# A linear-attention block: z computed inside the G stage, one memset on another engine, and one weight load in two parts

## The chip, the cores and the metric

The kernel runs on one core of one Trainium2 chip. The metric is the time of one execution on the device, in microseconds (us); less is better. A kernel counts as faster or slower only from 2% on (about 4.2 us here).

The engines are named as in the profile: PE is TensorE (PEld its weight loads), DVE is VectorE, ACT is ScalarE, POOL is GpSimd, and SP is SyncE, which here only issues DMA transfers. ACT issues a few DMA transfers too; its queue appears in the profile as q10, that of SP as q1.

## The reference

For x of 2048 x 640 in bf16 the result is the sum of three terms: x, a linear attention over the layer norm of x, and a two-layer GELU network over the same layer norm.

```python
def attention(x, wqkv, wo):           # H = 32 heads of Dh = 20
    q, k, v = ...                     # x @ wqkv, split by head
    phi = lambda t: jnp.where(t > 0, t + 1, jnp.exp(t)) + 1e-6
    pq, pk = phi(q), phi(k)
    kv  = jnp.einsum("bhsd,bhse->bhde", pk, v)
    z   = jnp.einsum("bhsd->bhd", pk)              # sum of phi(k) over the tokens
    num = jnp.einsum("bhqd,bhde->bhqe", pq, kv)
    den = jnp.einsum("bhqd,bhd->bhq", pq, z)[..., None] + 1e-6
    return (num / den).transpose(...).reshape(B, S, D) @ wo

def network(x, w1, b1, w2, b2):       # F = 1536
    return gelu(x @ w1 + b1) @ w2 + b2

xn = layernorm(x)
out = x + attention(xn, wqkv, wo) + network(xn, w1, b1, w2, b2)
```

## The kernel before

The kernel writes its instructions down through a small planner: `Pl.ins(engine, function, reads, writes)`. From the reads and writes the planner works out which semaphores each instruction waits for. Each engine runs its instructions in the order in which they were written down. `take(n)` hands out PSUM banks in a ring of eight; whoever takes a bank waits until its last reader is done.

The order of the stages on PE is: filler matmuls on zeros while the first loads arrive; W1 products with GELU (layer 1 of the network); K (with phi on ACT and DVE); G, the product of xn and phi(K), in five blocks f; Q chunk 0; z; KVT; Q chunks 1 and 2; M = KVT x Wo; Q chunk 3; then the output stage.

The loads at the start. W1 comes in four quarters of 480 KB; the first is issued on ACT's queue, the others on SP's, between the tiles of x:

```python
        dma_x(0, 1)                                                   # SP
        dma_w("scalar", b1tmp[:], B_b1.rearrange("(a p) -> a p", p=P), r_b1tmp)
        dma_w1(0, "scalar")                                           # first W1 quarter, ACT queue
        dma_x(1, 1)
        dma_w1(1)                                                     # second W1 quarter, SP queue
        dma_x(2, 1)
        dma_w1(2)
        # ... (cut)
```

The first products of layer 1, for token tile 0. They come in two groups: k = 0, 1 first, then k = 2, 3, 4. Both groups wait for the whole first quarter of W1:

```python
        def h_first(jbs):
            bs = [take(1) for _ in jbs]
            for (ks, res) in (((0, 1), r_xnTA), ((2, 3, 4), r_xnT[0])):
                for jb, b in zip(jbs, bs):
                    Pl.ins("tensor", [...matmuls for k in ks...],
                        reads=[r_W1[jb * P // FW], res], writes=[B_[b]])
            # ... (GELU, cut)
```

From the end of K to M. `KVT` and `GTb` lie in the memory of W1, so the memset and the G copies wait until layer 1 has read W1:

```python
        Pl.ins(v, lambda e: e.memset(KVT, 0.0), writes=[r_KVT] + r_W1)     # v is VectorE
        for f in range(DT):
            b = take(2)
            # ... 32 matmuls of G block f, and its copy to GTb on ScalarE (cut)

        # token sum on VectorE: zsum = PK[0] + PK[1] + ... + PK[15], fp32, then split in two bf16 parts zhl
        # ... (cut; 15 adds, a cast, a subtraction)

        q_chunk(0)
        z_step()      # 10 matmuls with N = 1; then DVE copies z and makes five ZB tiles
        kvt_step()    # 25 matmuls; then DVE masks and evicts five KVT tiles
        q_chunk(1)    # 5 units: 5 matmuls each, exp on ACT, then two DVE instructions (phi)
        q_chunk(2)
        m_step()      # 5 pairs of banks, 16 matmuls each, evicted by ACT
        q_chunk(3)
```

## Time and profile before

| What | Where it is read | Value |
|---|---|---|
| time, median of 3 runs | the runs | 210.89 us (210.71 to 210.95) |
| span of the profiled run | page | 209.0 us |
| PE busy | page | 204.9 us (98%) |
| first W1 products start | PE timeline | 6.84 us |
| first W1 quarter lands | DMA issues | 5.2 us after its issue at 1.46, so 6.7 |
| z products | chain | 0.36 us at 109.24 |
| M products, 80 matmuls | PE timeline | 121.91 to 125.67 = 3.76 us |
| token sum ends | DVE timeline | 99.92 us |

From the page of the kernel before: the busy time of each engine, and the chain of work that ended last.

```profile
PE 204.9 (98%) x1599; PEld 141.0 (67%) x1599; DVE 108.8 (52%) x227; ACT 75.1 (36%) x142; POOL 20.2 (10%) x61
...
PE 92%; DVE 6%; issue 1%; DVEq 0%
```

PE is almost always busy and makes up almost the whole chain. A change to another engine can only gain where that engine makes PE wait. The only such place inside the kernel is around M. Here is the PE timeline from the end of Q chunk 2 (columns: start, duration, engine, line, operation, tensors, shape, count, and in brackets the idle time before it and what ended it):

```profile
121.91 1.29 PE L545 MATMUL ps<-Wo,W 128*32 128x320 bf16 x32
123.38 0.75 PE L545 MATMUL ps<-Wo,W 128*32 128x320 bf16 x16 [0.18 <-DVE PQ L466]
124.38 1.29 PE L545 MATMUL ps<-Wo,W 128*32 128x320 bf16 x32 [0.24 <-DVE PQ L466]
125.60 2.57 PE L509 MATMUL ps<-xnT,Wqkv 128*128 128x512 bf16 x11
```

Eighty M matmuls (L545) come in three runs with gaps between them. The first 32 and the last 32 take 1.29 us each, that is 0.040 us for one, so 80 without a gap would take 3.22 us. They take 3.76, so about 0.54 us is lost. The releaser is the phi eviction on DVE (L466), which frees the banks. DVE is behind because z and KVT were put before its phi work. The chain in order of time (start, duration, what) shows it:

```profile
109.24 0.36 PE ps L517 x10
109.61 1.29 PE ps L529 x20
...
110.92 0.17 DVE z_sb L521
...
111.11 0.24 DVE ZB L523
...
112.42 0.22 DVE W L533
...
114.28 0.21 DVE ek L464
...
123.54 0.70 DVE PQ L466
...
124.38 1.29 PE ps L545 x32
```

After the z products (L517) and the KVT products (L529) it is DVE that goes on without a break: z copy, five ZB products, five KVT evictions (L533), ten phi pairs (L464 and L466), up to the last M matmuls.

At the start of the kernel, PE runs from the fillers (L298) over the transposes (L375, L303) into the first W1 products (L385) without a wait for a DMA:

```profile
6.34 0.45 PE L375 MATMUL ps<-ident,xn_tm 128*128 128x128 bf16 x3
6.73 0.18 PE L303 MATMUL ps<-ident,b1tmp 12*128 12x12 bf16 x1
6.84 1.22 PE L385 MATMUL ps<-xnT,W 128*128 128x128 bf16 x15
```

The quarter of W1 landed at about 6.7 us and was wanted at 6.84.

### The profile page before, as it was taken

Reading aid. Unit: us, or ns where it says so; the run is one execution under the profiler, and the core shown is the slowest. Engines: PE = TensorE matmul, PEld = TensorE weight load, DVE = VectorE, ACT = ScalarE, POOL = GpSimd, SP = SyncE. Lnnn points to the kernel's source line nnn. Section 1 sums busy time; section 2 is a strip of 40 time slices with the busy share of each in tenths; the row PEclk is TensorE's granted clock in tenths of the full one; section 3 lists DMA queues with packets and bytes.
Section 4 is the critical chain, followed back from the end, with each engine's and each line's share of the span. In section 5 each row is a group of like instructions: output and inputs, shape, how many; then the busy total and the mean of one; then the engine's idle time right before and its main releaser. Section 6 shows DMA issues by size and latency. Waiting matters only on the chain.

```text
span 209.0 us, 3950 instructions
## 1 busy us (share of the span) xinstructions
PE 204.9 (98%) x1599; PEld 141.0 (67%) x1599; DVE 108.8 (52%) x227; ACT 75.1 (36%) x142; POOL 20.2 (10%) x61
## 2 busy tenths in 40 slices
PE   7999999999999999999999999999999999999995
PEld 2799987444457777777756565577777777777775
DVE  4589970000008888999178975478633522523322
ACT  2689887666676444111253576100000000000000
POOL 3245568200000000000000000000000000000000
DMA  6999668997000000000000000591120111001001
GB/s 164 348 349 112 105 129 130 376 332 260 3 0 0 0 0 3 0 3 0 0 0 5 0 0 3 193 313 57 63 59 32 58 42 55 31 31 35 31 34 61
DMA packets 22507, 17.86 MB, mean 85 GB/s; under 512 B 9176, under 2 KB 22488, under 8 KB 22488
## 3 DMA queue, kind: packets, MB, share of 16 engines
q1 hardware_dynamic: 21808, 17.11, 29.1%
q10 hardware_dynamic: 680, 0.49, 0.9%
q8 instruction: 12, 0.20, 0.4%
q14 instruction: 7, 0.06, 0.1%
HBM read 12.62 MB, written 2.62 MB: 73 GB/s over the span
## 4 chain that ended last, share of the span: by engine, by line
PE 92%; DVE 6%; issue 1%; DVEq 0%
PE ps L617 33%; PE ps L355 25%; PE ps L487 10%; PE ps L476 10%; PE ps L509 5%; DVE PQ L466 3%; PE ps L298 2%; PE ps L653 2%; DVE ek L464 1%; DVE W L533 1%; PE ps L529 1%; PE ps L545 1%; DVE ZB L523 1%; PE ps L555 1%; PE ps L385 1%
## 5 line engine op out<-in xcount | busy, mean ns | idle before, releaser
L355 PE MATMUL ps<-xnT,W 128*128 128x128 bf16 (+2 forms) x435 | 52.0, 282 | 0.0
L617 PE MATMUL ps<-W,HG 128*128 128x320 bf16 x360 | 51.4, 299 | 0.0
L355 PEld LDWEIGHTS ps<-xnT,W 128*128 128x128 bf16 x435 | 35.6, 98 | 15.6
L617 PEld LDWEIGHTS ps<-W,HG 128*128 128x128 bf16 x360 | 35.1, 98 | 14.2 <-issue 0.4
L359 ACT ACTIVATE HG<-ps,b1c 128x128 bf16<-128x128 f32 (+2 forms) x87 | 40.1, 493 | 12.4 <-PE ps L355 10.3
L464 DVE TENSOR_SCALAR ek<-ek 128x512 bf16<-128x512 bf16 (+1 forms) x36 | 11.0, 305 | 42.7 <-ACT ek L463 41.6
L636 DVE TENSOR_TENSOR out_sb<-ps,xnT 128x640 bf16<-128x640 f32 x15 | 12.4, 825 | 36.2 <-PE ps L617 36.1
L463 ACT ACTIVATE ek<-ps 128x512 bf16<-128x512 f32 (+1 forms) x36 | 23.2, 645 | 20.4 <-PE ps L509 11.2
L617 PE MATMUL ps<-Msb,PQ 128*128 128x320 bf16 x150 | 22.5, 299 | 0.0
L509 PE MATMUL ps<-xnT,Wqkv 128*128 128x512 bf16 x100 | 22.1, 379 | 0.0
L476 PE MATMUL ps<-Wqkv,xnT 128*128 128x320 bf16 x160 | 21.9, 299 | 0.0
L487 PE MATMUL ps<-xPK,xn_tm 128*128 128x320 bf16 x160 | 21.9, 299 | 0.0
L476 PEld LDWEIGHTS ps<-Wqkv,xnT 128*128 128x128 bf16 x160 | 15.7, 98 | 6.2
L487 PEld LDWEIGHTS ps<-xPK,xn_tm 128*128 128x128 bf16 x160 | 15.7, 98 | 6.1
L617 PEld LDWEIGHTS ps<-Msb,PQ 128*128 128x128 bf16 x150 | 14.6, 98 | 5.7
L509 PEld LDWEIGHTS ps<-xnT,Wqkv 128*128 128x128 bf16 x100 | 11.6, 117 | 9.6 <-issue 0.2
L466 DVE SCALAR_TENSOR_TENSOR PQ<-ps,ek 128x512 bf16<-128x512 f32 x20 | 13.8, 692 | 2.1
L311 DVE BATCH_NORM_STATS2 stats<-xPK 128x6 f32<-128x320 bf16 x32 | 13.6, 466 | 2.3 <-DMA xPK<-in_A_x_dram 2.3
L466 DVE SCALAR_TENSOR_TENSOR xPK<-ps,ek 128x640 bf16<-128x640 f32 x16 | 13.2, 824 | 1.7
L497 DVE TENSOR_TENSOR Msb<-Msb,xPK 128x640 f32<-128x640 f32 x14 | 11.6, 825 | 0.5
L491 ACT ACTIVATE W<-ps 128x640 bf16<-128x640 f32 x5 | 3.5, 704 | 18.2 <-PE ps L487 14.6
L321 POOL TENSOR_TENSOR rstd<-aggr,mhalf 128x1 f32<-128x1 f32 x16 | 9.1, 568 | 8.9 <-DVE aggr L319 8.9
(68 smaller groups left out, 93.7 us busy)
## 6 DMA issues: line engine op xcount, KB each, us to landing
xnT<-in_A_x_dram SPq DMA_DIRECT2D x4, 640.0 KB, 6.2
Wqkv<-in_A_wqkv_dram SPq DMA_DIRECT2D x3, 800.0 KB, 6.7
out_dram<-out_sb SPq DMA_DIRECT2D x15, 160.0 KB, 1.8
W<-in_B_w_dram SPq DMA_DIRECT2D x1, 1920.0 KB, 15.3
W<-in_B_w_dram SPq DMA_DIRECT2D x3, 480.0 KB, 7.0
xPK<-in_A_x_dram SPq DMA_DIRECT2D x2, 640.0 KB, 9.5
Wo<-in_A_wo_dram SPq DMA_DIRECT2D x1, 800.0 KB, 10.5
xPK<-in_A_x_dram SPq DMA_DIRECT2D x4, 160.0 KB, 4.2
```

The lines of the kernel that those rows point to most:

```text
L311: Pl.ins(v, lambda e: e.bn_stats(stats[:, s, 6 * h:6 * h + 6], x_in[:, t, h * HW:(h + 1) * HW]), reads=[r_x[t]], writes=[r_stats[s][h]])
L355: Pl.ins("tensor", [(lambda e, k=k: e.matmul(bank(b, 0, w), W1[:, k, jb * P:(jb + 1) * P], xnT[:, k, tok], start=(k == 0), stop=(k == DT - ...
L359: Pl.ins("scalar", lambda e: e.activation(HG[:, jb, tok], bank(b, 0, w), ACT.Gelu_apprx_tanh, bias=b1c[:, jb:jb + 1]), reads=[B_[b], r_b1c ...
L463: Pl.ins("scalar", lambda e: e.activation(e2, src, ACT.Exp), reads=br, writes=[r_ek[s]])
L464: Pl.ins(v, lambda e: e.tensor_scalar(et, et, 1.0, 1e-6, ALU.min, ALU.add), reads=[r_ek[s]], writes=[r_ek[s]])
L466: Pl.ins(v, lambda e: e.scalar_tensor_tensor(out=d2, in0=src, scalar=0.0, in1=e2, op0=ALU.max, op1=ALU.add), reads=br + [r_ek[s]], writes= ...
L476: fns.append(lambda e, k=k, h=h, b=b, t=t: e.matmul(bank(b + h, 0, HW), xnT[:, k, t * P:(t + 1) * P], Wqkv[:, k, D + h * HW:D + (h + 1) * ...
L487: Pl.ins("tensor", [(lambda e, t=t, h=h, b=b, f=f: e.matmul(bank(b + h, 0, HW), xn_tm[:, t, f * P:(f + 1) * P], PK[:, t, h * HW:(h + 1) * ...
L497: Pl.ins(v, lambda e, t=t: e.tensor_tensor(out=zsum, in0=zsum, in1=PK[:, t, :], op=ALU.add), reads=[r_PK[t], r_zsum], writes=[r_zsum])
L509: Pl.ins("tensor", [(lambda e, k=k, j=j, b=b: e.matmul(bank(b), Wqkv[:, k, j:D:DT], xnT[:, k, cc], start=(k == 0), stop=(k == DT - 1))) fo ...
L617: return lambda e: e.matmul(bank(b + h, 0, HW), l, r[:, h * HW:(h + 1) * HW], start=(i == 0), stop=(i == JT + DT - 1))
L636: Pl.ins(v, lambda e: e.tensor_tensor(out=halves(out_sb[:, s, :]), in0=pair(b), in1=halves(x_res[:, t, :]), op=ALU.add), reads=B_[b:b + 2] ...
```

## The change

It wants to (1) take the z work out of DVE's way before M, by computing z inside the G stage, ahead of the last G block; (2) make the token sum end early enough for that, by zeroing KVT on GpSimd instead of VectorE; (3) start the first W1 products earlier, by loading the first W1 quarter as two DMA transfers, k = 0, 1 first.

```diff
+        r_W1a = R_("W1_0a")
...
-        dma_w1(0, "scalar")
+        dma_w("scalar", W1[:, 0:2, 0:FW], w1v[:, 0:2, 0:FW], r_W1a)
+        dma_w("scalar", W1[:, 2:DT, 0:FW], w1v[:, 2:DT, 0:FW], r_W1[0])
         dma_x(1, 1)
         dma_w1(1)
...
-                        reads=[r_W1[jb * P // FW], res], writes=[B_[b]])
+                        reads=[r_W1a if res is r_xnTA else r_W1[0], res], writes=[B_[b]])
...
-        Pl.ins(v, lambda e: e.memset(KVT, 0.0), writes=[r_KVT] + r_W1)
+        Pl.ins(g, lambda e: e.memset(KVT, 0.0), writes=[r_KVT] + r_W1)
...  (z_step and the token sum are now defined here; their instructions are unchanged)
+        token_sum()
         for f in range(DT):
             b = take(2)
+            zbank = (b + 3) % 8        # z_step uses this bank and takes none from the ring
+            if f == DT - 1:
+                z_step()
...
         q_chunk(0)
-        z_step()
         kvt_step()
```

## The prediction

> **What bounds the kernel now.** TensorE: the page gives PE 98% busy, the chain that ended last is 92% PE. DVE is on that chain only from 110.9 to 124.2 us. By stretches, PE is unbroken from 6.9 to 121.8 us; its one gap is 121.8 to 125.6 (3.38 busy of 3.80), the M products. Most of what the change touches limits nothing.
>
> **The wait at stake.** Chain: KVT products end at 110.90; then DVE without a break: z copy 0.17, five ZB products (to 112.42), five KVT evictions (to 114.28), ten phi pairs at 0.997 us to 124.24. PE supplies a phi unit every 1.08 us, so DVE starts late and has not caught up when the M products need the banks. These, 80 matmuls, last 121.91 to 125.67 = 3.76 us; the first and last 32 took 1.29 each, so without waits 80 take 3.22. Stall: about 0.54 us (the waits name 0.4, on the phi eviction).
>
> **Parts, costed.**
> 1. *z earlier.* 1.5 us of DVE work moves from 110.9 to about 100, where DVE is idle (5.67 us before 105.59). KVT evictions then start near 111 and phi near 112.8, not 114.2; phi follows PE's supply and ends near 123.4, about when the fourth M pair wants its bank. Stall left: 0 to 0.1. Gain 0.4 to 0.55 us. The ten z matmuls (0.36 us of PE) are moved, not removed. The bank ring loses one take, but pairs shift by two, so later conflicts stay.
> 2. *Is z ready?* The token sum ends at 99.92; PE reaches the fifth G block at 82.11 + 4 x 4.346 = 99.49. Without the DVE memset (1.39 us at 84.43) it ends near 98.6: no PE stall. The memset move makes this possible; alone it is worth nothing.
> 3. *GpSimd memset.* From 512 bf16 in 0.526 us and 140 in 0.215 I estimate 2.8 us for 3200, from 60.4 (last reader of W1) to 63.2; nothing needs it before 86.5. The Trainium skill ("SBUF — State Buffer", Who interferes with whom) says that a VectorE op in a 2-port mode and GpSimd block each other fully; the first such op starts at 63.16, so at most tenths, absorbed (phi takes 1.16 us of DVE per 1.36 of PE).
> 4. *W1 quarter in two.* The 480 KB on the ACT queue land 5.2 us after issue at 1.46, so about 6.7; the first products start at 6.84, held by the transposes ahead of them, not by W1: gain 0 to 0.1. The second part is needed at 7.38 and should land at 6.7 to 7.1: the skill ("DMA: Bandwidth & Descriptors", Queues, rings and completion order) says that each DMA engine takes turns between queues by packet, so splitting inside one queue should not change its share. The extra issue (0.4 us) delays ACT before its table load; ACT is next needed at 6.83. Net -0.1 to +0.2.
>
> **Sum.** 210.89 - 0.5 = 210.4 us; 8 in 10 between 209.9 and 210.8. Faster by over 2%: 0.01; within 2%: 0.98; slower by over 2%: 0.01.
>
> **What would show it.** z products between 99.4 and 100 without a PE gap; M products within 3.2 to 3.35 us; KVT evictions from about 111; a GpSimd memset of about 2.8 us near 60.4; first W1 products still at 6.8 to 6.9; output stage unchanged.
>
> **What would make it wrong.** The second W1 DMA landing after 7.4 (PE waits, +0.3 or more); the memset holding up DVE for microseconds; the token sum not ending before 99.5; an M pair still waiting.

## The result, and the profile after

Ratios below are computed as the mean time of one kernel's fast runs over the mean of the other's in the same rounds, so they are not quite the ratio of the medians quoted.

| | before | after |
|---|---|---|
| runs | 6 | 6 |
| median, us | 210.87 | 211.2 |
| lowest to highest, us | 210.71 to 211.03 | 210.3 to 215.13 |
| all runs, us | 210.95 210.89 210.71 211.03 210.85 210.75 | 213.84 215.13 210.89 210.3 211.44 210.97 |
| mean granted clock of the two runs above 213 | none | 0.992 (213.84), 0.984 (215.13) |

Fast runs against fast runs the ratio is 1.0002, with a 95% interval of 0.998 to 1.0023: the same. But the changed kernel scatters over 4.8 us, where the kernel before scatters over 0.3. The lowest run, 210.3, is the predicted time almost exactly; the others lie above it by 0.6 to 4.8 us. The prediction, 209.9 to 210.8, does not hold the median.

The profiled run was one of the long ones. In the changed kernel the M products are L553, the z products L490, the G matmuls L516, the W1 products L387 and L357, the memset L485. The part that the prediction was about went as predicted. PE around M:

```profile
125.46 3.27 PE L553 MATMUL ps<-Wo,W 128*32 128x320 bf16 x80
128.66 0.63 PE L528 MATMUL ps<-xnT,Wqkv 128*128 128x512 bf16 x2
```

All 80 M matmuls in one piece, 3.27 us. The z products (L490) run ahead of the last G block, and the chain has no gap around them (start, duration, what):

```profile
85.67 17.39 PE ps L516 x128
103.06 0.36 PE ps L490 x10
103.42 4.37 PE ps L516 x32
```

From the first K matmul to the last eviction of the chain it was 206.68 - 60.38 = 146.30 us before and is 209.74 - 63.94 = 145.80 us now: 0.50 us gained.

The start is where the time came back, and more. From the page, busy times and chain, in answer to those of before:

```profile
PE 206.0 (97%) x1599; PEld 142.4 (67%) x1599; DVE 107.9 (51%) x226; ACT 75.3 (36%) x142; POOL 22.9 (11%) x62
...
PE 91%; DVE 4%; DMA 3%; ACTq 0%; issue 0%; DVEq 0%
```

DMA has entered the chain with 3%, and DVE fell from 6 to 4%. The PE timeline at the start shows where:

```profile
6.42 0.18 PE L305 MATMUL ps<-ident,b1tmp 12*128 12x12 bf16 x1
6.56 0.49 PE L387 MATMUL ps<-xnT,W 128*128 128x128 bf16 x6
9.31 1.14 PE L387 MATMUL ps<-xnT,W 128*128 128x128 bf16 x9 [2.26 <-DMA W<-in_B_w_dram]
10.25 0.74 PE L341 MATMUL ps<-ident,xn_tm 128*128 128x128 bf16 x5
```

The second group of W1 products (L387, x9) starts at 9.31 us, after 2.26 us in which PE waited for the second part of the W1 quarter. The chain from the second group of W1 products on (L385 and L355 before, L387 and L357 after; start, duration, what), first of the kernel before, then of the changed one:

```profile
7.38 0.68 PE ps L385 x9
...
8.34 3.60 PE ps L355 x55
...
15.52 1.51 PE ps L355 x27
```

```profile
1.90 7.37 DMA W<-in_B_w_dram
...
9.31 1.14 PE ps L387 x9
...
10.99 4.50 PE ps L357 x55
...
19.07 0.95 PE ps L357 x17
```

Before, the large stretch of layer 1 (the last piece of each view; its length and count are cut off there by the end of the view's window) is reached at 15.52 us, after at 19.07: 3.55 us later. The wait explains 9.31 - 7.38 = 1.93 us of this. The other 1.62 us lie in the matmuls after the wait: nine W1 products take 1.14 us where they took 0.68, five transposes (left out above) 0.53 where they took 0.28, the 55 products after them 4.50 where they took 3.60. The table of stretches shows why (columns: stretch, then length, busy time and instruction count of each engine, then the granted clock of PE, the DMA share and GB/s):

```profile
core 0: us, PE busy (x) PEld busy (x) DVE busy (x) ACT busy (x) POOL busy (x), PEclk, DMA share, GB/s
9.30:11.00 1.70, 1.69 (x17) 1.69 (x18) 0.00 (x0) 1.01 (x3) 0.00 (x0) 0.51 1.09 347
11.00:15.50 4.50, 4.50 (x59) 4.38 (x58) 2.81 (x8) 3.34 (x10) 1.55 (x4) 0.81 1.07 360
```

For 1.7 us after the wait the mean granted clock was 0.51, in the next 4.5 us 0.81. The clock record of the trace says where it changed: it was half from 9.33 to 12.75 us, for 3.41 us, and full on either side. The same columns for these 3.41 us and the 3.41 us before them:

```profile
5.92:9.33 3.41, 1.15 (x14) 0.67 (x13) 0.82 (x3) 0.56 (x2) 0.21 (x1) 1.00 1.03 337
9.33:12.74 3.41, 3.41 (x33) 3.41 (x34) 1.61 (x5) 1.85 (x6) 0.25 (x2) 0.50 1.08 351
```

Half of 3.41 us is 1.7 us (an estimate of the loss), close to the 1.62 found above. In the kernel before the clock was 1.00 from 7.4 to 13.6 us. 3.55 us lost at the start, less 0.50 gained at M, makes 3.05, and the spans differ by 212.0 - 209.0 = 3.0 us.

So the profiled run is explained by its own trace. Two questions were open. Is the late second part the change's doing or chance? And why does it land so late, when it was issued only 0.4 us after the time at which the whole quarter used to be issued?

### The profile page after: what moved, and what is told of

The parts are those of the page before. It is cut to its first block, busy times and chain, and to the rows that moved or that the text cites. A ratio compares the mean times of both kernels' runs of the same rounds, so it can differ in the third digit from the quotient of the medians.

```text
span 212.0 us, 3973 instructions
## 1 busy us (share of the span) xinstructions
PE 206.0 (97%) x1599; PEld 142.4 (67%) x1599; DVE 107.9 (51%) x226; ACT 75.3 (36%) x142; POOL 22.9 (11%) x62
## 4 chain that ended last, share of the span: by engine, by line
PE 91%; DVE 4%; DMA 3%; ACTq 0%; issue 0%; DVEq 0%
PE ps L624 33%; PE ps L357 25%; PE ps L516 10%; PE ps L478 10%; PE ps L528 7%; DMA W<-in_B_w_dram 3%; DVE PQ L468 3%; PE ps L660 2%; DVE ek L466 1%; PE ps L537 1%; PE ps L553 1%; PE ps L563 1%; PE ps L387 1%; PE ps L341 1%; ACTq L235 0%
## 5 line engine op out<-in xcount | busy, mean ns | idle before, releaser
L357 PE MATMUL ps<-xnT,W 128*128 128x128 bf16 (+2 forms) x435 | 52.9, 286 | 0.0
L357 PEld LDWEIGHTS ps<-xnT,W 128*128 128x128 bf16 x435 | 36.6, 100 | 15.6
L516 PE MATMUL ps<-xPK,xn_tm 128*128 128x320 bf16 x160 | 22.1, 299 | 0.0
L516 PEld LDWEIGHTS ps<-xPK,xn_tm 128*128 128x128 bf16 x160 | 15.6, 98 | 6.0
```

The source lines that it names most:

```text
L357: Pl.ins("tensor", [(lambda e, k=k: e.matmul(bank(b, 0, w), W1[:, k, jb * P:(jb + 1) * P], xnT[:, k, tok], start=(k == 0), stop=(k == DT - ...
L516: Pl.ins("tensor", [(lambda e, t=t, h=h, b=b, f=f: e.matmul(bank(b + h, 0, HW), xn_tm[:, t, f * P:(f + 1) * P], PK[:, t, h * HW:(h + 1) * ...
```

## The experiments

Theory A: the second W1 transfer lands late, because it is issued after the SP queue has issued its own W1 quarter and shares the DMA engines with it; the wait that this makes eats what z gains, and where it is long PE also loses its clock. Rivals: the z move itself brings the scatter (B); two transfers cost more than one by themselves, whatever the order (A2); landing times are chance, whatever the queue (A3). In the first round A and B were set against each other, in the second the order against A2 and A3, in the third the low clock.

All outputs are right. The table gives every time measured, with how many of the runs had a mean granted clock below 0.998; the last column is from the profiled execution alone.

| kernel | runs | mean | lowest to highest | low clock | PE's wait for the first W1 quarter |
|---|---|---|---|---|---|
| after (first set) | 6 | 212.09 | 210.30 to 215.13 | 2 | 2.26 |
| after_again | 6 | 212.17 | 210.39 to 213.92 | 3 | 1.95 |
| one_dma | 6 | 210.26 | 209.99 to 210.72 | 0 | 0.95 |
| split_only | 6 | 212.26 | 210.80 to 214.14 | 2 | 0.45 |
| z_dve_memset | 6 | 211.44 | 210.58 to 213.41 | 1 | 1.46 |
| memset_only | 5 | 210.86 | 210.73 to 210.99 | 0 | below 0.2 |
| late_single | 6 | 213.32 | 211.68 to 214.70 | 4 | 1.73 |
| late_again | 6 | 213.99 | 211.83 to 215.43 | 5 | 1.60 |
| late_fill | 6 | 212.97 | 212.37 to 213.66 | 0 | 0.56, after 2.12 of filler |
| w1b_sp | 6 | 210.51 | 210.23 to 210.93 | 0 | none |
| sp_order | 5 | 210.12 | 209.89 to 210.31 | 0 | none |
| before_sp | 6 | 210.72 | 210.53 to 210.83 | 0 | none |
| sp_again | 6 | 210.14 | 209.91 to 210.58 | 0 | none |

The kernel before, run next to each of the three groups, had means of 210.86, 210.93 and 210.94 (11 runs each, lowest 210.44, highest 211.28 but for one run of 212.74 with a clock of 0.992).

A run is called slow here when it is over 1.5% above the fastest of the same kernel. With one core there is no other die to compare with, so the label says nothing of the cause, and some runs at 0.992 carry the label fast.

### one_dma: the change without the split

```diff
-        dma_w("scalar", W1[:, 0:2, 0:FW], w1v[:, 0:2, 0:FW], r_W1a)
-        dma_w("scalar", W1[:, 2:DT, 0:FW], w1v[:, 2:DT, 0:FW], r_W1[0])
+        dma_w1(0, "scalar")
-                        reads=[r_W1a if res is r_xnTA else r_W1[0], res], writes=[B_[b]])
+                        reads=[r_W1[jb * P // FW], res], writes=[B_[b]])
```

> The change with the W1 quarter loaded by one DMA again (z and memset stay). Theory A (the second W1 DMA lands late and eats the gain of z): first W1 products at 6.8 to 6.9 without a wait on W1, M products 3.2 to 3.35 us, time 210.3 to 210.45 in all runs, none slow, spread below 0.3 us; ratio to before about 0.9977. Rival B (the z move itself brings the slow runs or gains nothing): 210.9 or more, or some runs above 213.

Measured: 209.99 to 210.72, median 210.22, none at a low clock, ratio to before 0.9971 (0.9958 to 0.9984). M products 3.27 us. B falls: with z moved and the split undone, the gain is there, and in these six runs the scatter is gone. (It is not gone for good: z_dve_memset below, with the same single transfer, has one run of 213.41 at a clock of 0.992.) One part of the expectation was wrong: in the profiled run (210.72) the quarter did not land at 6.7 but 6.1 us after its issue at 1.45, and PE waited 0.95 us. Even one transfer lands late at times.

### split_only: the kernel before with the split alone

```diff
-        dma_w1(0, "scalar")
+        dma_w("scalar", W1[:, 0:2, 0:FW], w1v[:, 0:2, 0:FW], r_W1a)
+        dma_w("scalar", W1[:, 2:DT, 0:FW], w1v[:, 2:DT, 0:FW], r_W1[0])
-                        reads=[r_W1[jb * P // FW], res], writes=[B_[b]])
+                        reads=[r_W1a if res is r_xnTA else r_W1[0], res], writes=[B_[b]])
```

> The kernel before with only the W1 quarter in two DMAs. Theory A: second part lands after 7.4 us (up to about 9.3), PE waits for W1; times scatter from 210.9 to over 215, mean about 0.5 us or more above before, and M products still 3.7 us. Rival B: 210.9 in all runs, W1 not waited for.

Measured: 210.80 to 214.14, median 211.92; the ratio to before is 1.0061 (1.0019 to 1.0104), in which 213.88, labelled fast, counts although its clock was 0.992. The four runs at full clock have a mean of 211.39, 0.53 us above the 210.86 of before. In the profile the second part landed at 7.5 us and PE waited 0.45; that was the fastest of the six runs. The scatter comes with the split and without z. In the change, the loss of about 0.5 at full clock happens to be as large as the gain of about 0.5 from z: by this chance the ratio of the fast runs came out at 1.0002.

### after_again: the changed kernel a second time

No edit.

> The changed kernel once more, for a second profile and five more times. Theory A: times scatter by 1 us or more (210.3 to 215), the landing of the second W1 DMA in the profile differs from 9.27 us and the span of this profile follows it: span about 208.5 plus the wait for W1 plus the time lost at the lower clock. Rival B: same time as one_dma.

Measured: 210.39 to 213.92, three of six runs at a low clock; the three others have a mean of 210.75. In this profile the second part landed 7.6 us after its issue, PE waited 1.95 us and started the second group at 9.52. The stretch from there to the large stretch of layer 1 lasted 19.28 - 9.52 = 9.76 us, the same as 19.07 - 9.31 = 9.76 in the first profile, and 1.62 longer than before. The span was 212.2 us, and the expected sum is 208.5 + 1.95 + 1.62 = 212.1. The scatter repeats.

### z_dve_memset and memset_only: what the engine of the memset is worth

The first is one_dma with the memset back on VectorE, the second is the kernel before with the memset on GpSimd. The edit is the same line in both, in opposite directions:

```diff
-        Pl.ins(g, lambda e: e.memset(KVT, 0.0), writes=[r_KVT] + r_W1)
+        Pl.ins(v, lambda e: e.memset(KVT, 0.0), writes=[r_KVT] + r_W1)
```

> As one_dma, but the KVT memset back on DVE (token sum starts 1.3 us later). The token sum then ends near 99.9 us and PE, which reaches the z products at about 99.5, waits 0.4 to 0.5 us: time about 210.75, 0.4 us above one_dma. If the memset's engine does not matter: equal to one_dma within 0.1 us.

> The kernel before with the KVT memset on GpSimd and nothing else. It should gain nothing: 210.9, ratio 0.999 to 1.001, M products still about 3.7 us, token sum ending 1.3 us earlier; the memset about 2.8 us on GpSimd.

Measured: z_dve_memset has a mean of 211.04 over its five runs at full clock, against 210.26 for one_dma: 0.78 more, where 0.4 was expected. The PE timeline of z_dve_memset shows the wait; the z products are L489 and stood idle for the token sum on DVE (L505):

```profile
102.52 0.56 PE L489 MATMUL ps<-onesb,Msb 128*128 128x1 bf16 x10 [0.48 <-DVE Msb L505]
102.94 2.33 PE L515 MATMUL ps<-xPK,xn_tm 128*128 128x320 bf16 x16
```

From the first K matmul to the start of the output stage's last tile it takes 204.71 - 62.92 = 141.79 us, and in one_dma 202.03 - 60.92 = 141.11: 0.68 us. Of this, 0.42 is the time by which the sum comes too late (17.81 us after K's end, where PE arrives after 17.39), 0.05 passes until PE starts, and the z products then take 0.56 us where the chain of one_dma has 0.36. The direction is as expected, the size was taken too small. The rest of the 0.78 may be the scatter of W1, which this kernel keeps.

memset_only: 210.73 to 210.99, ratio 0.9996 (0.9984 to 1.0008). M products from 122.17 to 125.96 with both gaps, 3.79 us. The token sum ended at 98.57 instead of 99.92, and nothing waited for it. So the memset on GpSimd is worth nothing alone and 0.7 to 0.8 us under the z move: it is a condition for the gain and no gain of its own. It took 2.77 us there, on VectorE 1.39:

```profile
60.79 2.77 POOL L483 MEMSET W<- 128x3200 bf16 x1 [22.36 <-PE ps L355]
```

and in the kernel before:

```profile
84.43 1.39 DVE L483 MEMSET W<- 128x1600 uint32 x1 [0.28 <-issue]
```

The Trainium skill ("VectorE: DVE Perf Modes", Zero memsets can be issued as uint32) says that a VectorE memset takes a cycle per element, and that a zero memset of 2-byte elements can go out as half as many uint32. The trace agrees on the form: the row of VectorE has 1600 uint32 for the 3200 bf16, and the row on GpSimd, which has 3200 bf16, takes twice as long. No run here has the bf16 form on VectorE, so none shows what the uint32 form saves there.

### late_single: one transfer, issued just after SP's

The kernel before, with one more small load on ACT's queue ahead of the W1 quarter, so that the quarter is issued a little later (the cut leaves out the new tile and the b1 transpose, which waits for the extra load too):

```diff
+        dma_w("scalar", b1dup[:], B_b1.rearrange("(a p) -> a p", p=P), r_b1dup)
         dma_w1(0, "scalar")
```

> The kernel before (W1 quarter in one DMA), with a second copy of the small b1 load issued on the ACT queue ahead of it, so that the quarter is issued about 0.6 us later, after the SP queue has issued its own W1 quarter. Theory A1 (being issued behind the SP queue's W1 load is what makes it land late): lands at 8.5 to 9.5 us, PE waits 2 us or more, some runs at a clock of 0.992, mean 212 or more. Rival A2 (two DMAs cost more than one, by themselves): landing moves by the 0.6 us of issue only, 7.2 to 8.4, mean 211.0 to 211.5.

The issue moved by less than planned, from 1.46 to 1.79 us, but that was enough: SP issued its W1 quarter at 1.72. The landing moved to 8.6 us in the profile, PE waited 1.73 (2 or more was expected), and the mean was 213.32, with four of six runs at a low clock. A2, which allowed a mean of 211.0 to 211.5, falls: there is only one transfer, it was issued 0.33 us later, and the time rose by more than in the split kernels. (The landing alone would not decide: in late_again below, the same kernel, it was 8.1 us, which A2 allows.) What is left is the order: which of the two W1 transfers is issued first. One small doubt stays: the extra load of 3 KB is itself ahead of the quarter in ACT's queue, and no run had it there with the quarter still issued first. The DMA queues between 3 and 5 us (columns: queue and kind, packets, MB, share of the 16 engines' time), first of the kernel before, then of late_single:

```profile
DMA packets 629, 0.48 MB, mean 240 GB/s; under 512 B 17, under 2 KB 629, under 8 KB 629
...
q10 hardware_dynamic: 505, 0.38, 76.7%
q1 hardware_dynamic: 124, 0.10, 15.7%
```

```profile
DMA packets 569, 0.44 MB, mean 219 GB/s; under 512 B 33, under 2 KB 569, under 8 KB 569
...
q1 hardware_dynamic: 446, 0.36, 78.4%
q10 hardware_dynamic: 123, 0.08, 14.4%
```

ACT's queue (q10) moved 505 of 629 packets when its quarter was issued first, and 123 of 569 when it was issued 0.07 us after SP's. In the changed kernel, from 4 to 7 us, when the second part should have come in, ACT's queue moved 370 packets and SP's (q1) 648:

```profile
q1 hardware_dynamic: 648, 0.52, 65.7%
q10 hardware_dynamic: 370, 0.27, 28.1%
```

That is nearly the share that ACT's queue had in the kernel before in the same 3 us, 418 packets to 807. The difference is in the end of the transfer: after 7 us ACT's queue had no packet left to move in the kernel before, but 62 of its 696 in the changed kernel, and up to 9.3 us these came among 911 of SP's. It is the last tenth of the load that makes it land late.

The prediction leaned on the Trainium skill ("DMA: Bandwidth & Descriptors", Queues, rings and completion order), which says that each DMA engine takes turns between the queues packet by packet. A packet there is a group of descriptors, typically 9 to 17 and at most 64, drained from one queue before the next has its turn. The profile may count something smaller: in its trace the quarter is 640 packets of 768 bytes, 40 for each of 16 engines (an estimate), and one packet of the page could hold many of these. So uneven counts over 2 us neither confirm even turns nor speak against them, and no run shows the turns themselves.

### w1b_sp: the second part on SP's queue, ahead of SP's own quarter

```diff
         dma_w("scalar", W1[:, 0:2, 0:FW], w1v[:, 0:2, 0:FW], r_W1a)
-        dma_w("scalar", W1[:, 2:DT, 0:FW], w1v[:, 2:DT, 0:FW], r_W1[0])
         dma_x(1, 1)
+        dma_w("sync", W1[:, 2:DT, 0:FW], w1v[:, 2:DT, 0:FW], r_W1[0])
         dma_w1(1)
```

> The changed kernel with the second W1 part issued on the SP queue, ahead of that queue's own W1 quarter. A1: it lands before 7.4 us, PE hardly waits for W1, no run at a lower clock, time 209.9 to 210.3. A2: still late (8 us or more) in some runs, times scatter up to 213.

Measured: 210.23 to 210.93, mean 210.51, none at a low clock; the part landed 4.1 us after its issue, where it had taken 7.4, and all fifteen first W1 products ran without a wait, from 6.48 us on. So two transfers are not late as such: this one, ahead of SP's quarter, was under way for 3 us less. (It changed its queue too; that the order counts on one and the same queue rests on late_single.) Four of the six runs, up to 210.93 and one of them by 0.01 only, are above the expected 209.9 to 210.3. The profile shows a wait of 0.16 us for the second quarter instead; whether that is all of it, one profile cannot say.

### sp_order, before_sp and sp_again: one transfer, in order, in one queue

sp_order is one_dma with the first quarter on SP's queue, ahead of the second. before_sp is the same edit on the kernel before. sp_again is sp_order once more, on the same chip as before_sp.

```diff
-        dma_w1(0, "scalar")
         dma_x(1, 1)
+        dma_w1(0)
         dma_w1(1)
```

> As one_dma, but the whole first W1 quarter goes to the SP queue, third after two x tiles and ahead of the second W1 quarter; it is issued about 0.3 us later than in one_dma. A1 (sharing with and order against the SP queue's loads decides): it lands at 6.2 to 6.9 in spite of the later issue, against 7.5 and 8.0 in the two profiles with one DMA and memset or z changes; time 209.9 to 210.2 with a spread below 0.3 us. Rival A3 (landing is just late by chance, whatever the queue): as one_dma, 210.0 to 210.7, landing 6.7 to 8.

> The kernel before with only the issue order changed: first W1 quarter in one DMA on the SP queue, after two x tiles and ahead of the second quarter. If order and sharing decide the landing: no wait for W1, first W1 products at 6.5 to 6.9, time 210.5 to 210.7 with a spread of at most 0.3 us (before scatters over 0.8), M products still 3.7 us. The z part is absent, so about 0.5 us above sp_again. Rival: if the order is worth nothing, 210.9 as before.

> sp_order once more, beside before_sp on one chip: 209.9 to 210.3, all runs at clock 1.0, ratio to before 0.996 to 0.997, 0.4 to 0.55 us below before_sp (the z part alone).

Measured: sp_order 209.89 to 210.31, ratio 0.9961 (0.9948 to 0.9973); sp_again 209.91 to 210.58, ratio 0.9961 (0.9929 to 0.9993); before_sp 210.53 to 210.83, ratio 0.9989 (0.9961 to 1.0018). The highest run of sp_order is 0.1 above what was expected, that of sp_again 0.3, and four of the six of before_sp are up to 0.13 above. The last two ratios count the run of before at 212.74, whose clock was 0.992; without it before has a mean of 210.76, so that sp_again is 0.3% below it and before_sp level with it. The median of before_sp, 210.76, is not lower than the 210.79 of before on that chip; what it lacks is the tail of before, whose eleven runs there include 211.21 and 212.74. So the order does not make the kernel faster when all goes well; it seems to keep it from getting slower: before_sp keeps within 0.30 us, though six runs are few for something seen once in eleven. The z part alone, sp_again against before_sp, is 210.72 - 210.14 = 0.58 us; 0.4 to 0.55 was expected.

The PE timeline of sp_order at the start:

```profile
6.40 0.18 PE L304 MATMUL ps<-ident,b1tmp 12*128 12x12 bf16 x1
6.51 1.22 PE L386 MATMUL ps<-xnT,W 128*128 128x128 bf16 x15
7.57 0.44 PE L340 MATMUL ps<-ident,xn_tm 128*128 128x128 bf16 x5
```

Fifteen W1 products in one piece at 6.51 us, with no wait for W1, although the quarter was issued 0.3 us later than in one_dma. A3 falls for this load: in three profiles of three, with the quarter ahead of SP's, PE did not wait for it. What remains is that the second quarter now comes close: in sp_again PE's weight loads waited 0.3 us for it at about 8 us.

All runs together say more of the order than one kernel can. Where the quarter, or its second part, was issued behind SP's quarter (after, after_again, split_only, late_single, late_again), 16 of 30 runs had a low clock. Where it was ahead on ACT's queue (one_dma, z_dve_memset, memset_only and the 33 runs of before), it was 2 of 50, and ahead on SP's queue (w1b_sp, sp_order, before_sp, sp_again) none of 23.

sp_order is the version that beats both kernels: 0.4% below the kernel before, then 0.3 to 0.4%. It is under 2%, so it counts as the same. That it beats one_dma (ratio 0.9971, on another chip) is not shown.

### late_fill and late_again: is it the wait that lowers the clock?

late_fill is late_single with nine matmuls on zeros put where PE would wait. late_again is late_single once more, on the same chip.

```diff
         b1_step()
+        filler(9)
```

> late_single with nine extra 512-column matmuls on zeros (1.94 us of PE) put between the b1 transpose and the first W1 products, so that PE is not idle while W1 is on its way. If PE's idle time is what lowers the granted clock: clock 1.0 in all runs, time 211.3 to 212.8, about 1 us below late_again in its slow runs. Rival (the low clock comes of itself): clock 0.992 as often as in late_again, times up to 214.7.

> late_single once more, beside late_fill: mean near 213, about two in three runs at clock 0.992; runs at clock 1.0 between 211.5 and 212.5.

Measured: late_fill 212.37 to 213.66, all six at 0.999 or 1.000. late_again 211.83 to 215.43, five of six at 0.992 or below; those five have a mean of 214.42. In its profile the quarter landed as late as in the changed kernel, and PE had 0.56 us of idle time before it instead of 2.26. The PE timeline, and the stretches at the same times as those of the changed kernel above:

```profile
6.70 2.12 PE L301 MATMUL ps<-warm 128*128 128x512 bf16 x9
9.37 1.01 PE L388 MATMUL ps<-xnT,W 128*128 128x128 bf16 x15 [0.56 <-DMA W<-in_B_w_dram]
```

```profile
9.30:11.00 1.70, 1.63 (x29) 1.63 (x30) 0.30 (x1) 0.91 (x4) 0.00 (x0) 1.00 1.10 335
11.00:15.50 4.50, 4.50 (x65) 4.28 (x63) 3.42 (x11) 3.90 (x12) 1.55 (x4) 1.00 1.07 361
```

The clock stays at 1.00. So the low clock is not something that befalls the runs from outside: the idle time of PE at the start brings it. Three of the six times are above the expected range, up to 213.66. Nine fillers also hold PE back when W1 is early: the best run, 212.37, is above the 211.83 of late_again at full clock. The filler is a measuring tool here, not a remedy.

The length of the wait alone does not decide. In single profiles a wait of 1.46 us (z_dve_memset) was followed by a low clock, while waits of 1.60 and 1.73 (late_again, late_single) were not followed by any loss. The clock records in the traces say more. In the three profiles with a low clock it was half for one step of 3.41 us: from 9.33 us (after), 10.12 (after_again) and 7.86 (z_dve_memset). In the 3.41 us that ended there PE was busy for only 1.15, 1.46 and 1.57 us; z_dve_memset had another gap, of 0.62 us, in them. The records of the profiles without a loss run in the same steps (their first entry lasts 204.8 us, 60 steps). In the step that holds the wait PE was busy for 1.68 us (late_single), 1.81 (late_again), 2.12 (one_dma) and 2.37 (split_only). So in these seven profiles the three with the least PE work in one step lost half the clock in the next. Seven profiles do not place the limit, and the same wait can cost the clock or not, depending on where the steps fall.

This also fits with the few sizes in which the low clock comes. A mean of 0.992 over 212 us is a loss of 0.008 x 212 = 1.7 us, one step at half the clock, and 0.984 would be two (estimates; no profile has a clock of 0.984). The 18 low-clock runs here have 0.991, 0.992 or 0.984.

## Why the prediction was wrong, point by point

- **PE bounds the kernel, and only M has a wait inside it: right.** M products went from 3.76 to 3.27 us (predicted 3.2 to 3.35).
- **z earlier gains 0.4 to 0.55: right.** 0.50 by the traces of before and after; 0.58 by runs of sp_again against before_sp.
- **z is ready in time because the memset left VectorE: right.** The z products started at 103.06 in the profile after, which is 17.39 us after the end of K (85.67), without a gap. With the memset on VectorE PE waits and 0.7 to 0.8 us are lost.
- **The GpSimd memset takes 2.8 us and disturbs nothing: right.** 2.76 us, from 64.08 to 66.84. The skill's rule that GpSimd and a 2-port VectorE instruction block each other ("SBUF — State Buffer", Who interferes with whom) was hardly put to the test: VectorE's first instruction of that stage started at 66.71, as late after the first K matmul as before (2.77 and 2.78 us), and took 0.33 us as before. The two spans overlap by 0.13 us, and spans on POOL are rough, so no run here shows the rule or a breach of it.
- **The W1 quarter in two, "Net -0.1 to +0.2": this is the step that failed.** The prediction said that the second part "should land at 6.7 to 7.1". It landed at 9.27, 9.47 and 7.5 us in three profiles with the split. In the profiled run this term of the sum was 3.55 us, of which 1.93 was the wait and 1.62 the clock; at full clock it is about 0.5 us (split_only against before), which is the whole gain of z. Two things were missed. First, the argument was about the share of a queue, which hardly changed (36% of the packets against 34% from 4 to 7 us), while the load landed 2.6 us later; what counted was the order of issue against the other queue's W1 transfer, and the split moved 288 KB from ahead of SP's first W1 quarter to behind it, for a first part that nobody had waited for. Second, the risk was named ("PE waits, +0.3 or more") and kept out of the range, and the loss of clock that can follow a wait was not named at all.
- **A reading that was too sure.** "Held by the transposes ahead of them, not by W1" was true of the one execution in the profile. The same load landed 5.2, 5.5, 6.1 and 6.6 us after its issue in four profiles with the transfer as in the kernel before. PE's own arrival moved too: where it did not wait, the first W1 products started between 6.48 us (w1b_sp) and 7.06 (after_again). A margin of 0.2 us read from one profile was no margin, and the 0.24 us by which three runs of before differed was no measure of it either: of 33 later runs, 32 lay between 210.44 and 211.28, and one was 212.74.

## What to carry to other kernels

A transfer whose margin is a few tenths of a microsecond in one profile has none: look at how the times of many runs scatter, and do not push its bytes behind another queue's transfer in the order of issue. Splitting a load helps only if something waits for the first part, and it moves the second part back in that order; at the start of a kernel the safe form was one queue, in the order in which the data is wanted. When PE waits near the start, count the clock that it loses as well as the wait: here 1.6 us on top of 1.9.

## What the Trainium skill lacked or had wrong

- "TensorE: Matmul & The Clock Gate", Why this matters for your kernels, advises against idle gaps of PE over about 3 us. Here gaps of 1.46, 1.95 and 2.26 us (z_dve_memset, after_again, after) were followed by half the clock for 3.41 us; against the kernel before, 1.62 us were lost in each of the two profiles of the changed kernel. Gaps of 1.60 and 1.73 us cost nothing in two other profiles. What went with the loss was PE's busy time in one step of 3.41 us: 1.57 us or less before a loss, 1.68 or more where there was none.
- "DMA: Bandwidth & Descriptors", Queues, rings and completion order, describes the DMA engines as taking turns between queues by packet, and does not say what this means for the end of a transfer as small as these. Between 3 and 5 us ACT's queue moved 505 of 629 packets when its W1 quarter was issued 0.27 us before SP's, and 123 of 569 when it was issued 0.07 us after; in the changed kernel the last 62 of its 696 packets came after 7 us, and the load landed at 9.27.
- The same page, Issuing engines are not separate DMA queues, says that starting transfers from several engines only saves issue time. That they interleave agrees; what is missing is that the order of issue across engines went with the order of landing: in all seven profiles with a whole W1 quarter on each queue the one issued first landed first. The quarter that PE needs first was 5.2 to 6.6 us under way when issued first, and 6.4 to 7.5 when issued 0.06 or 0.07 us after the other.
- No page gives the scatter of one and the same transfer from run to run: 480 KB under way for 5.2, 5.5, 6.1 and 6.6 us in four profiles with the same order of issue.
